# More products on zeros, and v products streamed twice, in the first batch of a fused attention and FFN kernel

## The chip, the cores and the metric

The kernel runs on one core of one Trainium2 chip. The metric is the device time of one execution in microseconds (us), the median over several executions. A profile of one execution tells how its time is spread over the engines: TensorE (PE, with its weight loads shown apart as PEld), VectorE (DVE), ScalarE (ACT), GpSimd (POOL) and the DMA queues that SyncE (SP) and POOL issue.

## The reference

For 4 batches of 8 heads with 768 positions of width 64, an 8x8 matrix per head is normalised by five rounds of exp, row sum and column sum (Sinkhorn). It mixes blocks of 96 keys and of 96 values: these are the "sorted" k and v. Each block of 96 queries then attends to its sorted block, and the result goes through a feed-forward net with squared ReLU.

```python
P = sort_net
for _ in range(5):
    P = np.exp(P - np.max(P, axis=-1, keepdims=True))
    P = P / (np.sum(P, axis=-1, keepdims=True) + 1e-09)
    P = P / (np.sum(P, axis=-2, keepdims=True) + 1e-09)
k_sorted = np.einsum('bhij,bhjcd->bhicd', P, k_b)
v_sorted = np.einsum('bhij,bhjcd->bhicd', P, v_b)
attn = softmax(scale * q_b @ k_sorted.T)          # per block of 96
x = (attn @ v_sorted) as [B * S, H * D]
out = (s * relu(x @ w_in) ** 2 + b) @ w_out
```

## The kernel before, in words

All work is written out in one order by hand (a manual schedule), and each engine runs its instructions in that order. A batch has two tiles of 384 positions, t = 0 to 7 over the four batches.

PSUM is shared by two pools of rotating buffers: `psa`, three buffers of two banks, and `psb`, two buffers of one bank. A new tile of a pool takes over a buffer, and its first write waits until all work on the tile that held it before is over.

The start of the program is about batch 0:

- `warm_up(n)` issues n matmuls of a 128x128 block of zeros with 256 columns of zeros (tile `zt`) into tiles `wp` of `psb`, one new tile for each. Nothing reads them.
- The Sinkhorn rounds run on DVE and ACT (lines 181 to 201).
- `q_half(half, eng)` transposes half of q of batch 0 on TensorE (`tq`, L244) and evicts it to `qt` on ACT.
- `build_pd1` spreads the normalised matrix over partitions with one f32 product (`pe`, L213), then builds the block-diagonal matrix `pd1` on DVE.
- `k_piece` makes sorted k: products `tk` (L278), evicted to `ks` by DVE ("v") or ACT ("s").
- `v_piece0(d0, n, eng)` makes sorted v of batch 0: for each of n columns of the head dimension one product `tv` (L304) of a strided slice of `vb` (64 rows, 128 columns) with the 64 columns of `pd1`, each into its own 64 columns of PSUM; then one eviction to `vs`.
- `s_piece(t, hp)` makes the scores of a head pair (`sc`, L359) and their exp on ACT (`at`, L362). `p_piece` multiplies them with v (`pv`, L386), and DVE divides (L390, L391) into `x`. `t_piece` transposes `x` (`tr`, L414) to `xt`.
- `ffn1` is the first FFN product (`hps`, L433) with its ReLU on ACT (L437) and square on DVE (L438); `ffn2` the second (`ops`, L459). Both call "slots" in between, in which pieces of the next batch are placed.

v of batch 1 takes another way: `v_piece1` multiplies, evicts to `vn` and writes to DRAM (`dv`, L326, on SP's queue); `v_read(1, nc.sync)` reads it back in another layout (`vs<-dv`, L345). The p pieces of tile 2, in a slot of `ffn2(0)`, are the first to need it. Loads of q, k, v and of the weights go by POOL's queue, each behind the last use of the buffer that it fills.

Of the kernel before, what the change touches and what calls it, by code (L numbers as in the profile page):

```python
# [9 lines left out]
FP = mybir.dt.float32  # L10
# [8 lines left out]
def kernel(  # L19
# [12 lines left out]
    nc = tc.nc  # L32
# [33 lines left out]
    psa = ctx.enter_context(tc.tile_pool(name="psa", bufs=3, space=bass.MemoryType.PSUM))  # L66
    psb = ctx.enter_context(tc.tile_pool(name="psb", bufs=2, space=bass.MemoryType.PSUM))
# [7 lines left out]
    vb = const.tile([128, 128, D], BF)  # L75
# [67 lines left out]
    for c0 in range(0, d_ff, FCH):  # L143
        w = const.tile([128, NHP, FCH], BF, name=f"wi{c0}")
        nc.gpsimd.dma_start(
            out=w, in_=moe_w_in.rearrange("(hp p) f -> p hp f", p=128)[:, :, c0:c0 + FCH])
# [19 lines left out]
    jsel = const.tile([128, NB], FP)  # L166
    ks = const.tile([128, 64, BLK], BF)

    def warm_up(n):
        for _ in range(n):  # L170
            wp = psb.tile([128, 256], FP, tag="b", name="wp")
            nc.tensor.matmul(out=wp, lhsT=zt[:, 0:128], rhs=zt, start=True, stop=True)  # L172

    def zero_pad(r0):
# [59 lines left out]
    def q_half(half, eng):  # L234

        if half == 0:
            QT[0] = qtp.tile([128, NHP, S], BF, tag="qt", name="qt0")
        pr = slice(half * 64, half * 64 + 64)
        ps = psa.tile([128, 2, 1024], BF, tag="a", name="tq")
        for hp in range(NHP):  # L240
            for t in range(TQ):
                c0 = (hp % 2) * TG + t * 64
                for e in range(2):
                    nc.tensor.transpose(out=ps[e * 64:(e + 1) * 64, hp // 2, c0:c0 + 64],  # L244
                                        in_=qr[0][pr, 2 * hp + e, t, :], identity=ident[pr, pr])
        for a in range(2):
            evac(QT[0][:, 2 * a:2 * a + 2, half * TG:(half + 1) * TG].rearrange(
                     "q b (p t) -> q b p t", t=TQ),
                 ps[:, a, 0:2 * TG].rearrange("q (b t p) -> q b p t", b=2, t=TQ), eng)
# [15 lines left out]
    def k_piece(b, c0, nc2, nb, eng):  # L265

        pr = brows(b)[1] if nb == 1 else slice(0, 128)  # L270
        rhs = (pd1[pr].rearrange("p e m i -> p (e m i)") if nb == 1
               else pd2.rearrange("p b e m i -> p (b e m i)"))
        if nc2 * nb > 8:
            ps = psa.tile([128, nc2, nb * 64], FP, tag="a", name="tk")
        else:
            ps = psb.tile([128, nc2, nb * 64], FP, tag="b", name="tk")
        for c in range(nc2):
            nc.tensor.matmul(out=ps[:, c, :],  # L278
                             lhsT=kb[pr, c0 + 2 * c:c0 + 2 * c + 2, :].rearrange("p c d -> p (c d)"),
                             rhs=rhs, start=True, stop=True)  # L280
        g0 = (b % 2) * 32

        def half(cp):
            if b == 0:
                cs = slice(c0 + cp, c0 + 2 * nc2, 2)
            else:
                cs = slice(cp * (BLK // 2) + c0 // 2, cp * (BLK // 2) + c0 // 2 + nc2)
            for e in range(2):
                evac(ks[e * 64:(e + 1) * 64, g0:g0 + nb * 32, cs].rearrange(
                         "p (b g) c -> p b g c", b=nb),  # L290
                     ps[cp * 64:(cp + 1) * 64].rearrange(
                         "p c (b e g) -> p e b g c", b=nb, e=2)[:, e], eng)

        half(0)
        return lambda: half(1)

    def v_piece0(d0, n, eng):

        if n > 8:
            ps = psa.tile([128, n, 64], FP, tag="a", name="tv")  # L300
        else:
            ps = psb.tile([128, n, 64], FP, tag="b", name="tv")
        for t in range(n):
            nc.tensor.matmul(out=ps[:, t, :], lhsT=vb[0:64, :, d0 + t],  # L304
                             rhs=pd1[0:64].rearrange("p e m i -> p (e m i)"),
                             start=True, stop=True)
        evac(VS[0][:, :, d0:d0 + n], ps[0:BLK].rearrange("p t g -> p g t"), eng)


# [40 lines left out]
    def s_piece(t, hp):  # L350

        b, half = divmod(t, 2)
        g0 = (b % 2) * 32 + hp * NB + half * HB
        sc = psa.tile([BLK, 2, 512], FP, tag="a", name="sc")
        for n in range(HB):
            for e in range(2):
                pr = slice(e * 64, (e + 1) * 64)
                q0 = (half * HB + n) * BLK
                nc.tensor.matmul(out=sc[:, e, n * BLK:(n + 1) * BLK], lhsT=ks[pr, g0 + n, :],  # L359
                                 rhs=QT[b][pr, hp, q0:q0 + BLK], start=True, stop=True)  # L360
        at = atp.tile([BLK, 2, TG], BF, tag="at", name="at")
        nc.scalar.activation(out=at, in_=sc[:, :, 0:TG], func=AF.Exp, scale=scale)  # L362
        AT[t, hp] = at

    def p_piece(t, hp, n0=0, nn=HB):

        b, half = divmod(t, 2)
        at = AT[t, hp]
        if t not in X:
            X[t] = xp.tile([BLK, HB, d_model], BF, tag="x", name="x")  # L370
        x = X[t]
        atf = at.rearrange("p e t -> p (e t)")
        if nn < HB:
            p1 = psb.tile([128, 512], FP, tag="b", name="pv")
            pv = [p1[:, e * nn * VW:(e + 1) * nn * VW] for e in range(2)]
            pvv = p1[0:BLK, 0:2 * nn * VW].rearrange("p (e n w) -> p e n w", e=2, w=VW)
        else:
            p2 = psa.tile([128, 2, 512], FP, tag="a", name="pv")
            pv = [p2[:, 0], p2[:, 1]]
            pvv = p2[0:BLK, :, 0:nn * VW].rearrange("p e (n w) -> p e n w", w=VW)  # L380
        for e in range(2):
            for n in range(n0, n0 + nn):
                c0 = (e * HB + n) * BLK
                m = 128 if c0 + 128 <= 2 * TG else BLK
                gi = e * 32 + hp * NB + half * HB + n
                nc.tensor.matmul(out=pv[e][0:m, (n - n0) * VW:(n - n0 + 1) * VW],  # L386
                                 lhsT=atf[:, c0:c0 + m],
                                 rhs=VS[b][:, gi, :], start=True, stop=True)
        rec = rtp.tile([BLK, 2, HB], FP, tag="rec", name="rec")
        nc.vector.reciprocal(out=rec[:, :, 0:nn], in_=pvv[:, :, :, D])  # L390
        nc.vector.tensor_tensor(  # L391
            out=x[:, n0:n0 + nn, hp * 128:(hp + 1) * 128].rearrange("p n (e d) -> p e n d", e=2),
            in0=pvv[:, :, :, 0:D],
            in1=rec[:, :, 0:nn].unsqueeze(3).broadcast_to([BLK, 2, nn, D]), op=ALU.mult)

    def t_piece(t, eng, n0=0, nn=HB):

        x = X[t]
        if t not in XT:
            XT[t] = xtp.tile([128, NHP, TG], BF, tag="xt", name="xt")  # L400
        if nn < HB:
            t1 = psb.tile([128, 1024], BF, tag="b", name="tr")
            tr = [t1[:, hp * nn * BLK:(hp + 1) * nn * BLK] for hp in range(NHP)]
            src = t1[:, 0:NHP * nn * BLK]
            dst = XT[t][:, :, n0 * BLK:(n0 + nn) * BLK]
            src = src.rearrange("p (a t) -> p a t", a=NHP)
        else:
            t2 = psa.tile([128, 2, 1024], BF, tag="a", name="tr")
            tr = [t2[:, hp // 2, (hp % 2) * TG:(hp % 2 + 1) * TG] for hp in range(NHP)]
            src = t2[:, :, 0:2 * TG]  # L410
            dst = XT[t].rearrange("p (a b) t -> p a (b t)", b=2)
        for hp in range(NHP):
            for n in range(n0, n0 + nn):
                nc.tensor.transpose(out=tr[hp][:, (n - n0) * BLK:(n - n0 + 1) * BLK],  # L414
                                    in_=x[:, n, hp * 128:(hp + 1) * 128],
                                    identity=ident[0:BLK, 0:BLK])
        evac(dst, src, eng)
# [91 lines left out]
    def build_pd1():  # L509
        pt = block_rows(0)  # L510
        nc.vector.tensor_tensor(  # L511
            out=pd1, in0=hmask.rearrange("p (m e) i -> p e m i", e=2),
            in1=bass.AP(tensor=pt.tensor, offset=pt.offset,
                        ap=[list(pt.ap[0]), [0, 2], [0, NHP], list(pt.ap[1])]),
            op=ALU.mult)
# [11 lines left out]

    warm_up(38)
    q_half(0, "s")
    warm_up(12)  # L530
    build_pd1()
    k_piece(0, 0, 16, 1, "v")()
    k_piece(0, 32, 16, 1, "s")()
    k_piece(0, 64, 8, 1, "v")()
# [3 lines left out]
    v_piece0(32, 16, "v")  # L538
    s_piece(0, 0)
    s_piece(0, 1)  # L540
    v_piece0(48, 16, "v")
    s_piece(0, 2)
    s_piece(0, 3)
    q_half(1, "s")
    for hp in range(NHP):
        p_piece(0, hp, 0, 2)
    t_piece(0, "v", 0, 2)
    s_piece(1, 0)
    s_piece(1, 1)

# [105 lines left out]
```

The softmax here doesn't subtract the row's maximum and nothing guards it: scores larger than these inputs give would overflow.

## Time and profile before

| what | value |
|---|---|
| median of 6 executions | 249.31 us (248.58 to 252.93) |
| the profiled execution's own time | 252.93 us |
| its span, first to last instruction | 251.2 us |
| mean granted TensorE clock | 0.952 |
| TensorE busy | 234.8 us (93%) |
| DVE, ACT busy | 133.3 us (53%), 116.4 us (46%) |

The profiled execution is the longest of the six. In the rows of the profile, a line such as "9.59 2.02 PE L172 MATMUL wp<-zt 128*128 128x256 bf16 x12" is: start in us from the span's start, length of the group in us, engine, line of the kernel, operation, tile written and tiles read, rows and columns of the weights, shape that streams, and the number of instructions. A bracket at its end gives the engine's idle time before the group and what ended it. In the forty slices of the page, a digit is a tenth: of busy time for an engine, of full speed for the granted clock (PEclk; 9 is 0.9 or more).

### The profile page before, as it was taken

To read this page: it belongs to the slowest core of one execution; us is meant where nothing else is said; L and a number is where in the kernel's file an instruction comes from. 1 tells how busy PE (TensorE), PEld (TensorE's weight loads), DVE (VectorE), ACT (ScalarE), POOL (GpSimd) and SP (SyncE) were. 2 spreads that over 40 slices of the span, in tenths; PEclk is the share of its full clock that TensorE was granted. 3 is DMA by queue.
4 is the path that set the end of the run, shared out by engine and by line. 5 is a ranking of instruction groups with operands and counts; after the bars stand their busy time and mean duration, and the time that the engine had idled before them with its cause. 6 is when DMAs were issued, how large, how long until landed. Compare 5 with 4: busy or idle time off the path is not lost.

```text
span 251.2 us, 4978 instructions
## 1 busy us (share of the span) xinstructions
PE 234.8 (93%) x2128; PEld 141.4 (56%) x2128; DVE 133.3 (53%) x260; ACT 116.4 (46%) x156; POOL 39.3 (16%) x51
## 2 busy tenths in 40 slices
PE   8879799799999699989899999999999999999993
PEld 4578699645544355655555555665555555664441
DVE  4776556999991236547774535344364353442221
ACT  5346566335358153677754141666431536661000
POOL 7720200588800007200000000000000000000000
PEclk9955579999999799999999999999999999999999
DMA  4999999999759936995001121100012110000122
GB/s 62 188 195 212 213 201 206 207 207 232 135 116 121 316 125 69 154 153 90 0 1 44 51 77 42 44 0 0 4 42 82 46 68 18 3 0 35 49 83 85
DMA packets 20214, 24.97 MB, mean 99 GB/s; under 512 B 7520, under 2 KB 14432, under 8 KB 19680
## 3 DMA queue, kind: packets, MB, share of 16 engines
q0 software_dynamic: 8400, 15.21, 35.5%
q1 hardware_dynamic: 11792, 9.45, 14.6%
q8 instruction: 16, 0.26, 0.5%
q14 instruction: 6, 0.05, 0.1%
HBM read 29.63 MB, written 8.65 MB: 152 GB/s over the span
## 4 chain that ended last, share of the span: by engine, by line
PE 69%; DVE 12%; DMA 9%; ACT 6%; issue 1%; SPq 1%; DVEq 0%
PE ops L459 29%; PE hps L433 27%; DMA vs<-dv 5%; PE pv L386 4%; DVE gt L438 3%; DMA dv<-vn 3%; ACT rt L437 3%; PE sc L359 3%; PE tr L414 2%; ACT ks L230 2%; PE tv L304 2%; DVE ks L228 1%; DVE qt L228 1%; PE tk L278 1%; DMA sn<-in_sort_net_dram 1%
## 5 line engine op out<-in xcount | busy, mean ns | idle before, releaser
L459 PE MATMUL ops<-wo,gt 128*128 128x512 bf16 x384 | 91.6, 383 | 0.0
L433 PE MATMUL hps<-xt,wi 128*128 128x384 bf16 (+1 forms) x576 | 89.2, 311 | 2.4 <-ACT ks L230 1.1
L433 PEld LDWEIGHTS <-wi 128*128 128x128 bf16 x576 | 54.3, 99 | 31.7 <-issue 4.1
L437 ACT ACTIVATE rt<-hps 128x768 bf16<-128x768 f32 (+1 forms) x72 | 53.3, 740 | 38.1 <-PE hps L433 34.4
L438 DVE TENSOR_TENSOR gt<-rt 128x768 bf16<-128x768 bf16 (+1 forms) x72 | 43.0, 601 | 43.1 <-ACT rt L437 42.8
L459 PEld LDWEIGHTS <-gt 128*128 128x128 bf16 x384 | 35.3, 99 | 39.1 <-issue 1.7
L450 DVE SCALAR_TENSOR_TENSOR ot<-ops,s_bc,bias 128x512 f32<-128x512 f32 x24 | 18.0, 748 | 36.4 <-PE ops L459 36.4
L362 ACT ACTIVATE at<-sc 96x768 bf16<-96x768 f32 x32 | 24.2, 802 | 24.1 <-PE sc L359 24.1
L391 DVE TENSOR_TENSOR x<-pv,rec 96x512 bf16<-96x512 f32 (+1 forms) x36 | 22.6, 628 | 1.3
L230 ACT COPY xt<-tr 128x1536 bf16<-128x1536 bf16 x6 | 8.6, 1439 | 23.6 <-PE tr L414 23.6
L228 DVE CAST ks<-tk 64x512 bf16<-64x512 f32 (+1 forms) x28 | 18.6, 664 | 1.7 <-PE tk L278 1.3
L390 DVE RECIPROCAL rec<-pv 96x8 f32<-96x8 f32 (+1 forms) x36 | 6.9, 193 | 20.6 <-PE pv L386 20.6
L583 POOL TENSOR_TENSOR csum<-csum,wo 128x512 f32<-128x512 f32 x14 | 17.6, 1255 | 1.0
L230 ACT CAST ks<-tk 64x512 bf16<-64x512 f32 (+1 forms) x24 | 14.0, 582 | 7.1 <-PE tk L278 6.8
L386 PEld LDWEIGHTS <-at 96*128 96x128 bf16 (+1 forms) x256 | 12.2, 105 | 7.5 <-DMA vs<-dv 3.1
L386 PE MATMUL pv<-vs,at 96*128 96x66 bf16 (+1 forms) x256 | 13.1, 201 | 3.4 <-DMA vs<-dv 2.6
L359 PEld LDWEIGHTS <-ks 64*96 64x96 bf16 x256 | 8.4, 132 | 6.1 <-issue 5.0
L359 PE MATMUL sc<-qt,ks 64*96 64x96 bf16 x256 | 10.8, 223 | 0.3 <-DVE ks L228 0.2
L172 PE MATMUL wp<-zt 128*128 128x256 bf16 x50 | 9.7, 323 | 1.1 <-DVE warm L104 1.1
L230 ACT CAST vn<-tv 128x1024 bf16<-128x1024 f32 x6 | 6.1, 1012 | 8.5 <-PE tv L334 8.3
L345 POOL DMA_DIRECT2D vs<-dv x4 | 5.4, 1348 | 24.9 <-DMA dv<-vn 23.5
L278 PE MATMUL tk<-pd,kb 64*128 64x64 bf16 (+1 forms) x144 | 8.3, 216 | 0.9 <-DVE pd L511 0.9
(67 smaller groups left out, 120.6 us busy)
## 6 DMA issues: line engine op xcount, KB each, us to landing
out_dram<-ot SPq DMA_DIRECT2D x24, 256.0 KB, 2.0
kb<-in_k_dram POOLq DMA_DIRECT2D x4, 768.0 KB, 22.4
vb<-in_v_dram POOLq DMA_DIRECT2D x4, 768.0 KB, 19.3
qr<-in_q_dram POOLq DMA_DIRECT2D x3, 768.0 KB, 36.4
wi<-in_moe_w_in_dram POOLq DMA_DIRECT2D x2, 1024.0 KB, 18.9
wo<-in_moe_w_out_dram POOLq DMA_DIRECT2D x2, 1024.0 KB, 30.5
dv<-vn SPq DMA_DIRECT2D x6, 256.0 KB, 3.5
vs<-dv POOLq DMA_DIRECT2D x4, 384.0 KB, 11.2
```

The lines of the kernel that those rows point to most:

```text
L228: nc.vector.tensor_copy(out=out, in_=in_)
L230: nc.scalar.copy(out=out, in_=in_)
L359: nc.tensor.matmul(out=sc[:, e, n * BLK:(n + 1) * BLK], lhsT=ks[pr, g0 + n, :], rhs=QT[b][pr, hp, q0:q0 + BLK], start=True, stop=True)
L362: nc.scalar.activation(out=at, in_=sc[:, :, 0:TG], func=AF.Exp, scale=scale)
L386: nc.tensor.matmul(out=pv[e][0:m, (n - n0) * VW:(n - n0 + 1) * VW], lhsT=atf[:, c0:c0 + m], rhs=VS[b][:, gi, :], start=True, stop=True)
L391: nc.vector.tensor_tensor(out=x[:, n0:n0 + nn, hp * 128:(hp + 1) * 128].rearrange("p n (e d) -> p e n d", e=2), in0=pvv[:, :, :, 0:D], in1 ...
L433: nc.tensor.matmul(out=hps[:, f, 0:nt], lhsT=wi_at(hp, f0 + f), rhs=xt[:, hp, c0:c0 + nt], start=(hp == 0), stop=(hp == NHP - 1))
L437: nc.scalar.activation(out=rt[:, :, 0:nt], in_=hps[:, :, 0:nt], func=AF.Relu)
L438: nc.vector.tensor_tensor(out=gt[:, f0:f0 + 2, c0:c0 + nt], in0=rt[:, :, 0:nt], in1=rt[:, :, 0:nt], op=ALU.mult)
L450: nc.vector.scalar_tensor_tensor(out=ot, in0=ops, scalar=s_bc, in1=bias, op0=ALU.mult, op1=ALU.add)
L459: nc.tensor.matmul(out=ops, lhsT=gt[:, f, m * 128:(m + 1) * 128], rhs=wo_at(f), start=(f == 0), stop=(f == NF - 1))
L583: nc.gpsimd.tensor_tensor(out=csum, in0=csum, in1=wo_at(f), op=ALU.add)
```

## The change

Only batch 0's part, before the first `ffn1`, is touched. `warm_up` takes one tile for all its matmuls, of `psb` or, where asked, of `psa`. The number of matmuls on zeros grows: 22 instead of 12 after the first q half, 9 more between the f32 product of `build_pd1` and the first k piece, 6 before the last v piece, 6 before the second q half, and 2 in `psa` after each of the four p pieces and after the t piece. In `v_piece0` each product streams the 64 columns of `pd1` twice in a row (a broadcast access) and writes 128 columns of PSUM: its own 64 and the 64 of the next product, which then overwrites them. The last product of each eight streams once.

```diff
-    def warm_up(n):
+    def warm_up(n, pool=psb):
+        wp = pool.tile([128, 256], FP, tag="b" if pool is psb else "a", name="wp")
         for _ in range(n):
-            wp = psb.tile([128, 256], FP, tag="b", name="wp")
             nc.tensor.matmul(out=wp, lhsT=zt[:, 0:128], rhs=zt, start=True, stop=True)
...
         for t in range(n):
-            nc.tensor.matmul(out=ps[:, t, :], lhsT=vb[0:64, :, d0 + t],
-                             rhs=pd1[0:64].rearrange("p e m i -> p (e m i)"),
-                             start=True, stop=True)
+            r = 2 if t % 8 < 7 else 1
+            nc.tensor.matmul(out=ps[:, t:t + r, :], lhsT=vb[0:64, :, d0 + t],
+                             rhs=pd1[0:64].rearrange("p e m i -> p (e m i)").unsqueeze(1)
+                             .broadcast_to([64, r, 64]), start=True, stop=True)
...
     warm_up(38)
     q_half(0, "s")
-    warm_up(12)
+    warm_up(22)
     build_pd1()
+    warm_up(9)
     k_piece(0, 0, 16, 1, "v")()
     k_piece(0, 32, 16, 1, "s")()
...
     s_piece(0, 0)
     s_piece(0, 1)
+    warm_up(6)
     v_piece0(48, 16, "v")
     s_piece(0, 2)
     s_piece(0, 3)
+    warm_up(6)
     q_half(1, "s")
     for hp in range(NHP):
         p_piece(0, hp, 0, 2)
+        warm_up(2, psa)
     t_piece(0, "v", 0, 2)
+    warm_up(2, psa)
     s_piece(1, 0)
     s_piece(1, 1)
```

## The prediction

> **What bounds the kernel now.** I read the page's busy times and its forty slices first, then a table of the first 40 us in windows, then the timeline there, last the waits behind it. Page: TensorE is the bound over the span, and its clock is halved in slices 3 to 5 and partly in 14.
>
> ```profile
> PE 234.8 (93%) x2128; PEld 141.4 (56%) x2128; DVE 133.3 (53%) x260; ACT 116.4 (46%) x156; POOL 39.3 (16%) x51
> PEclk9955579999999799999999999999999999999999
> ```
>
> Windows: start and end, their length, each engine's busy time, and after the five engines the granted clock.
>
> ```profile
> 10.00:15.00 5.00, 3.21 (x36) 2.38 (x36) 2.61 (x13) 1.62 (x3) 2.12 (x3) 0.85 0.98 203
> 15.00:20.00 5.00, 4.34 (x60) 4.16 (x57) 4.84 (x9) 4.22 (x7) 0.54 (x1) 0.50 1.18 207
> 30.00:35.00 5.00, 5.00 (x60) 4.52 (x58) 1.83 (x6) 2.49 (x4) 0.88 (x1) 0.60 1.19 191
> 35.00:40.00 5.00, 5.00 (x81) 4.43 (x78) 3.70 (x13) 3.73 (x8) 0.00 (x0) 1.00 1.23 204
> ...
> 82.00:84.00 2.00, 0.01 (x1) 0.01 (x1) 0.00 (x0) 0.00 (x0) 0.00 (x0) 1.00 1.24 281
> 86.00:88.00 2.00, 2.00 (x6) 0.76 (x5) 0.23 (x1) 1.01 (x1) 0.00 (x0) 0.50 0.76 283
> ```
>
> A mean of 0.85 over 10 to 15 puts the fall at 13.5 (1.5 us at half); 0.60 over 30 to 35 puts the rise at 34.0. So all of batch 0 before the FFN runs at half clock, 20.5 us. A second, single stretch of about 3.4 us (85.2 to 88.6) follows a TensorE wait; 20.5 is six times 3.4, so I take it (estimate) that the clock is decided every 3.4 us on the 3.4 us before.
>
> Timeline: start, length, engine, line, operation, count, idle time before and what ended it.
>
> ```profile
> 9.59 2.02 PE L172 MATMUL wp<-zt 128*128 128x256 bf16 x12
> 12.49 0.40 PE L213 MATMUL pe<-sn,emat 32*128 32x64 f32 x2 [0.88 <-DVE sn L201]
> 13.80 2.71 PE L278 MATMUL tk<-pd,kb 64*128 64x64 bf16 x48 [0.90 <-DVE pd L511]
> 16.77 1.62 PE L304 MATMUL tv<-pd,vb 64*128 64x64 bf16 x16 [0.26 <-DMA vb<-in_v_dram]
> 18.80 2.96 PE L304 MATMUL tv<-pd,vb 64*128 64x64 bf16 x32 [0.40 <-ACT ks L230]
> 23.07 1.38 PE L304 MATMUL tv<-pd,vb 64*128 64x64 bf16 x14 [0.57 <-ACT at L362]
> 25.94 1.49 PE L244 MATMUL tq<-ident,qr 64*64 64x64 bf16 x48 [0.64 <-DVE vs L228]
> 28.58 0.38 PE L386 MATMUL pv<-vs,at 96*128 96x66 bf16 x4 [0.60 <-DVE rec L390]
> 31.32 1.46 PE L433 MATMUL hps<-xt,wi 128*128 128x192 bf16 x8
> 34.99 0.83 PE L433 MATMUL hps<-xt,wi 128*128 128x192 bf16 x8
> ...
> 83.99 0.71 PE L386 MATMUL pv<-vs,at 96*128 96x66 bf16 x16 [2.59 <-DMA vs<-dv]
> ```
>
> To be seen: eight FFN products take 1.46 us at half clock and 0.83 at full; TensorE's waits between 11 and 31 us are short (0.2 to 1.15) and end on DVE or ACT; and the end of batch 1's v (vs<-dv, back from DRAM) is the next place where TensorE stands still.
>
> **What makes the clock fall.** I counted, per 3.4 us, the time in which columns stream (columns over 2.4 per ns at full clock: cold wp start every 0.213 us for 256 columns, and half that warm). 10.1 to 13.5 has 9 wp of 0.107 and the f32 product, 33%: it falls. 81.8 to 85.2 has 32%: it falls. 47.6 to 51.0 has 49%: it stays. Cold, 13.5 to 16.9 has 77% and does not rise; 30.6 to 34.0 has 94% and rises. The Trainium skill (TensorE: Matmul & The Clock Gate, "Why this matters for your kernels") says the clock halves after gaps of over some 3 us between bursts, one idle window. By that rule no gap here is long enough (the longest before 13.5 is 0.9 us), nothing would fall, and filling short waits would be worth 0. The rows decide: a window one third full fell. I take 0.4 of streaming as the edge, between 0.33 and 0.49.
>
> **The change part by part.**
> *Warm-ups in one tile.* Now each wp takes a fresh buffer of two and waits for the product two before: 168 ns each warm (12 in 2.02), 202 over the 38. With one tile that wait goes; I take 107 to 110 warm (stream only), 213 cold (as now). If the rewriting of the same bank waited for each end instead, the price is a whole product, 269 ns warm and 371 cold by its rows: the upper bound, and a rival. I take the stream, since accumulating products (ops L459) rewrite one bank back to back with no wait. The 38 then end near 8.0 instead of 8.8 (26 cold to 6.7, 12 x 0.11), q half 0 starts 0.7 earlier (its load has landed by 7.2), and nobody needs it before ACT at 10.8: 0.
> *22 for 12, and 9 after pd's product.* 22 x 0.11 = 2.4 us, 8.95 to 11.35, before the Sinkhorn result at 12.4: hidden. Nine take 1.0 from 12.75 against pd at 13.75: hidden to within 0.1; cold they would be 1.9 and put 1.0 on the path. Windows now: about 60% in 10.1 to 13.5, about 50% in 13.5 to 16.9 (9 wp rest, 48 tk x 27 ns): above 0.4, so no fall.
> *k products.* 53 ns each now, 29 warm (16 in 0.64 at 66.6 us, less the last one's 0.19). Second piece ready 0.6 to 0.7 earlier; ACT's four evictions (15.70 to 18.75) move by that, so v's second piece starts at 18.2 (behind the first, which stays on its DMA at 16.77) instead of 18.80: -0.6.
> *v streamed twice.* 88 ns each now ((2.96 - 0.27)/31) although 64 columns stream in 53: the strided weight load bounds it. Doubled, 128 columns are 107 cold and 53 warm. Warm it hides under 88 (cost 0); if the load follows the clock, a product falls to about 54 and a piece gains another 0.5; cold, +19 ns x 16 = 0.3 a piece. I take 0 (no row shows this load warm). Its streaming share becomes 60% instead of 30%.
> *Six warm-ups before v's last piece and six before q half 1.* Warm 0.65 each in waits of 0.85 (22.2 to 23.07) and 0.9 (25.0 to 25.94): hidden. Cold 1.28: +0.45 each. With DVE's evictions 0.5 earlier, q half 1 starts near 25.45 (-0.5); its 48 transposes take 0.95 (as at 8.71) instead of 1.49: -1.1 at the first p piece.
> *Two warm-ups in psa after each p piece and after t.* 0.22 each. They take PSUM buffers of psa: by rotation the third needs q half 1's, which ACT empties 1.5 us after the transposes (27.9): p piece 3 waits about 0.2 more behind it. DVE's pace (0.55 a piece) hides the rest; bound 0 to 0.5, I take 0.2. First FFN product at about 30.3 instead of 31.32: -1.0.
> *FFN until 34.0.* Two rounds at 1.4 cold against about 0.9: -1.0.
> Sum: 2.0 us earlier at 34 us. The profiled execution rose as early as it could (the FFN filled the window from 30.6); where the decision falls later in that window the old kernel loses up to 1.7 more, +0.6 as an estimate. So 2.0 to 2.6.
> *What is late next.* From 34 to 81 TensorE is nearly always busy, so the shift goes through. POOL's loads of the next batches are issued earlier too, but the DMA engines are full until 67 (share about 1), so that moves nothing. Batch 1's v goes out in twelve writes, the last landing near 70.7 with the tail of the loads, and comes back in 13 us (70.8 to 84). If writes move with their issue, all of the gain stays; if they end with the loads, none does. Their latency (8.4 us) is a full queue's, which moves with the issue: I take 0.75 of 2.3 = 1.7.
>
> **Base.** The profiled execution is 252.93 us (span 251.2, 1.7 around it), 3.6 over the median of 249.31; its second clock stretch costs at most 1.7 of that. The stage changed precedes both, so I take the 1.7 off the median: 247.6.
>
> **Rivals.**
> A, *the clock falls all the same* (26%): if activity counts rows as well as columns, k and v products on 64 of 128 rows count half, and 16.9 to 20.3 would stand at 0.27 and 13.5 to 16.9 at 0.32, where 0.28 (the same count in 10.1 to 13.5) fell and 0.43 (47.6 to 51.0) stayed. The rows fit this as well as they fit columns. Then the wp run at 213 ns: +0.45 twice, v +0.3 twice, +0.5 to 0.9 around the p pieces, less 0.6 already gained and an earlier rise: +0.5 to +2, so 249.8 to 251.3, slower. It decides from a fall before about 24 us.
> B, *the wait at vs<-dv takes it* (17%): v's return stays at its time, TensorE idles 2 us longer before the p pieces of tile 2; 249.3, and where that wait leaves a window under 0.4, up to 1.7 of half clock more, 251.0. For: the last writes land with the last load (70.0). Against: latency as above.
> C, *rewriting a tile waits* (7%): 38 x 0.43 alone puts q half 0 at 17.4, v 64 x 0.2 more: over 260. Against: the accumulating rows.
> The forecast itself: 50%.
>
> **Numbers.** No change means within 0.2% (0.5 us), about what measuring this kernel can tell. Forecast: 246.3 to 248.7 on its own (v's load following the clock below, half the shift lost above). Faster: 0.50 plus a little of A and B where the rise comes early or half is lost, 0.52. Same: half of B and a part of A, 0.14. Slower: most of A, the rest of B, C, 0.34. Range 246.4 to 251.4: it leaves out C and thin ends.
>
> **What would show it.** Right: clock 1.0 from about 6.7 to the wait before tile 2's p pieces; tk in about 1.6 us; tv pieces of 16 still near 1.4; q half 1 in 0.95; first hps at 30.3; everything at 50 us two us earlier. Wrong: 0.5 anywhere in 13 to 30 (A); the same start of the pv at 84 with a longer idle before it (B); wp rows started over 250 ns apart (C).

## The result, and the profile after

The changed kernel takes 249.50 us (median of 34 executions, 248.19 to 251.47), the kernel before 248.98 us (71 executions, 247.84 to 253.30). The ratio is 1.0030, 95% interval 1.0015 to 1.0045: slower by 0.3%, where 0.7% faster had been forecast. Ratios, and the counts of executions by their clock below, leave out executions more than 1.5% above the fastest of the same kernel. The profiled execution of after took 249.45 us, with a span of 247.7 us. The 251.2 us span of the profile shown of before is at the long end of its executions, so a second trace of the kernel before (span 247.6 us, 249.3 us in all) is used below wherever times within the span are compared. It is called "before, second trace".

The page of after: busy time of each engine, and the granted TensorE clock in forty slices of 6.2 us.

```profile
PE 234.8 (95%) x2169; PEld 143.6 (58%) x2169; DVE 133.1 (54%) x260; ACT 116.3 (47%) x156; POOL 39.3 (16%) x51
PEclk9995599999999999999999999999999999999999
```

The clock still falls. The table of windows tells where (start and end, length, busy time of PE, PEld, DVE, ACT and POOL, then the granted clock, the DMA share and GB/s).

```profile
12.00:15.00 3.00, 2.72 (x54) 2.30 (x55) 1.25 (x4) 0.12 (x1) 0.88 (x1) 1.00 0.94 194
15.00:18.00 3.00, 1.36 (x23) 1.27 (x20) 2.91 (x6) 2.94 (x5) 0.54 (x1) 1.00 1.21 202
18.00:22.00 4.00, 4.00 (x51) 4.00 (x51) 2.64 (x5) 2.75 (x5) 0.00 (x0) 0.52 1.13 212
26.00:30.00 4.00, 4.00 (x72) 3.07 (x69) 1.37 (x3) 2.32 (x4) 1.09 (x3) 0.50 1.11 228
30.00:34.00 4.00, 3.96 (x56) 2.99 (x54) 2.50 (x8) 1.72 (x3) 0.85 (x1) 0.78 1.14 192
```

From 18 to 30 us TensorE is never idle, 4.00 of 4.00 in each window, and the clock is at half all the same. The trace's own clock records give the fall at 18.14 and the rise at 31.80. The timeline of the same stretch shows what TensorE did there:

```profile
8.10 2.58 PE L172 MATMUL wp<-zt 128*128 128x256 bf16 x22
12.31 1.16 PE L172 MATMUL wp<-zt 128*128 128x256 bf16 x9
13.74 1.57 PE L278 MATMUL tk<-pd,kb 64*128 64x64 bf16 x48 [0.28 <-DMA kb<-in_k_dram]
16.95 4.72 PE L306 MATMUL tv<-pd,vb 64*128 64x128 bf16 x46 [1.64 <-DMA vb<-in_v_dram]
22.43 1.46 PE L172 MATMUL wp<-zt 128*128 128x256 bf16 x6
23.82 1.68 PE L306 MATMUL tv<-pd,vb 64*128 64x128 bf16 x14
26.26 1.46 PE L172 MATMUL wp<-zt 128*128 128x256 bf16 x6
27.65 1.49 PE L244 MATMUL tq<-ident,qr 64*64 64x64 bf16 x48
29.29 0.62 PE L172 MATMUL wp<-zt 128*128 128x256 bf16 x2
33.14 0.82 PE L435 MATMUL hps<-xt,wi 128*128 128x192 bf16 x8
```

Three things are to be seen. The k products take 1.57 us instead of 2.71 (2.18 in the second trace), so they end 1.2 us sooner (0.65 against the second trace), and TensorE then stands still for 1.64 us because v's load lands where it did before (16.95, against 16.77 and 16.85). The two groups of six zeros run at half clock, 1.46 us each with the last one's tail, in places where the kernel before waits 0.57 and 0.64. And the first FFN product starts at 33.14 us.

Rows of before, second trace, for the same places:

```profile
13.78 2.18 PE L278 MATMUL tk<-pd,kb 64*128 64x64 bf16 x48 [0.90 <-DVE pd L511]
16.85 4.42 PE L304 MATMUL tv<-pd,vb 64*128 64x64 bf16 x48 [0.89 <-DMA vb<-in_v_dram]
22.53 1.42 PE L304 MATMUL tv<-pd,vb 64*128 64x64 bf16 x14 [0.57 <-ACT at L362]
25.43 1.49 PE L244 MATMUL tq<-ident,qr 64*64 64x64 bf16 x48 [0.64 <-DVE vs L228]
30.81 1.46 PE L433 MATMUL hps<-xt,wi 128*128 128x192 bf16 x8
```

Against these, each step comes out so (the last column is what the step added to after's lateness):

| start, us | before, second trace | after | step added |
|---|---|---|---|
| scores behind v's third piece | 21.08 | 21.37 | 0.29 |
| last v piece | 22.53 | 23.82 | 1.00, the first six |
| scores behind it | 23.67 | 25.20 | 0.24, v streamed twice |
| q half 1 | 25.43 | 27.65 | 0.69, the second six |
| first FFN product | 30.81 | 33.14 | 0.11, the pairs |
| 33rd FFN product | 35.97 | 36.81 | -1.49 |
| p pieces of tile 2 | 82.04 | 82.18 | -0.70 |

So 2.33 us are lost up to the FFN. 1.49 us come back there, since after's clock rises at 31.80 and the other's at 34.94; another 0.70 come back by tile 2, 0.54 of it a wait for batch 1's v that the kernel before has and after has not. The rows of tile 2, before (second trace) and then after:

```profile
82.04 0.71 PE L386 MATMUL pv<-vs,at 96*128 96x66 bf16 x16 [0.54 <-DMA vs<-dv]
```

```profile
82.18 0.70 PE L388 MATMUL pv<-vs,at 96*128 96x66 bf16 x16
```

What is left at tile 2 in these two traces is 0.14 us. Over all executions 0.5 us is left.

### The profile page after: what moved, and what is told of

Same layout as the page of the kernel before. It is cut to its first block, busy times and chain, and to the rows that moved or that the text cites. A ratio compares the mean times of both kernels' runs of the same rounds, so it can differ in the third digit from the quotient of the medians.

```text
span 247.7 us, 5058 instructions
## 1 busy us (share of the span) xinstructions
PE 234.8 (95%) x2169; PEld 143.6 (58%) x2169; DVE 133.1 (54%) x260; ACT 116.3 (47%) x156; POOL 39.3 (16%) x51
## 4 chain that ended last, share of the span: by engine, by line
PE 79%; DVE 8%; DMA 6%; ACT 4%; issue 1%; POOL 1%; POOLq 0%
PE ops L461 33%; PE hps L435 28%; DMA vb<-in_v_dram 6%; PE pv L388 4%; PE sc L361 3%; ACT rt L439 3%; PE tv L306 3%; DVE gt L440 2%; DVE ks L228 2%; PE tr L416 2%; PE wp L172 2%; DVE qt L228 1%; PE tq L259 1%; PE tv L336 1%; ACT ks L230 1%
## 5 line engine op out<-in xcount | busy, mean ns | idle before, releaser
L461 PE MATMUL ops<-wo,gt 128*128 128x512 bf16 x384 | 90.5, 379 | 0.0
L435 PE MATMUL hps<-xt,wi 128*128 128x384 bf16 (+1 forms) x576 | 88.0, 308 | 2.5 <-ACT ks L230 1.1
L435 PEld LDWEIGHTS <-wi 128*128 128x128 bf16 x576 | 53.4, 98 | 31.6 <-issue 4.1
L172 PE MATMUL wp<-zt 128*128 128x256 bf16 x91 | 15.5, 329 | 1.1 <-DVE warm L104 1.1
L172 PEld LDWEIGHTS <-zt 128*128 128x128 bf16 x91 | 9.7, 115 | 3.4 <-DVE warm L104 1.1
L228 DVE COPY qt<-tq 128x1536 bf16<-128x1536 bf16 x4 | 7.0, 1754 | 3.5 <-PE tq L259 3.5
L347 POOL DMA_DIRECT2D vs<-dv x4 | 5.4, 1348 | 20.5 <-DMA dv<-vn 19.1
```

Source lines behind the costliest of these rows:

```text
L228: nc.vector.tensor_copy(out=out, in_=in_)
L435: nc.tensor.matmul(out=hps[:, f, 0:nt], lhsT=wi_at(hp, f0 + f), rhs=xt[:, hp, c0:c0 + nt], start=(hp == 0), stop=(hp == NHP - 1))
L461: nc.tensor.matmul(out=ops, lhsT=gt[:, f, m * 128:(m + 1) * 128], rhs=wo_at(f), start=(f == 0), stop=(f == NF - 1))
```

## What the clock counts

In every trace the clock's changes lie on a grid of 3.413 us: 18.14 less 4.49 (after's first rise) is four times that. The Trainium skill (TensorE: Matmul & The Clock Gate, "What's actually happening") gives that window and says that it runs freely; here its phase against the program differs from trace to trace: where the clock rises at the start, it does so between 3.78 and 6.99 us.

For each such window I counted, from the instructions of a trace, the time in which a matmul streams: its columns divided by 2.4 per ns, or by 1.2 at half clock. Each product is weighted by the share of the array that its weights take: rows over 128 times columns over 128. Products that overlap in time (transposes, scores) add up in this array share; in the plain streaming time the overlap counts once. This count is my own; the profile has no such row. Over the first 100 us of after, both traces of before and the other 15 experiments, the array share parts the windows without one exception:

```
array share in a window   what the clock did at its end
full, 0.10 to 0.36        fell (22 windows)
full, 0.39 and more       stayed
half, up to 0.75          did not rise
half, 0.77 and more       rose
```

Streaming time without the rows, which is what the prediction counted, doesn't part them: windows fell at up to 0.56 and stayed at 0.44. Rows alone, with overlapping products added up, don't either: half-clock windows at 0.90 did not rise, others at 0.78 did. With overlap counted once, though, rows alone part the falls as well (0.36 fell, 0.39 stayed) and nearly part the rises (0.73 did not rise, 0.71 did). So the windows show that rows count; that the columns of the weights do is less certain. In after, the window from 14.73 to 18.14 holds the rest of k, the wait, and the start of v: 0.31 of streaming, 0.15 of the array. The next one, all v, streams 0.97 of the time at half clock but stands at 0.51 of the array, and doesn't rise.

## The experiments

The theories: R, a product counts by the rows and columns of its weights and the time it streams, so v on 64 rows stands too low even when it streams twice; C, streaming time alone counts, whatever the rows; H, the fall comes from the hole ahead of v's load alone; and for the end of the time, whether the return of batch 1's v gives back what was lost or won.

**Zeros in the hole.** To after, 16 zeros between k and v:

```diff
     k_piece(0, 80, 8, 1, "s")()
+    warm_up(16)
     v_piece0(0, 16, "v")
```

> The changed kernel with 16 more matmuls on zeros between the last k piece and the first v piece, where TensorE waited 1.6 us for v's load while the clock was still full. Theory R (activity counts rows as well as columns: 64 of 128 rows is half): the window that fell at 18.1 now holds about 0.7 and the clock stays up there, but the next one is v products alone (0.3 by rows and columns) and falls, near 21.5: TensorE's first FFN product at 32 to 33 us, time 0.999 to 1.003 of the kernel before. Theory C (columns alone count, the 1.6 us hole was all): v streamed twice holds 0.6, the clock stays full to 80 us, first FFN product near 30.3, time 0.990 to 0.995.

Measured: 1.0309 (1.0281 to 1.0337). The experiment put itself in the way. Its tile takes a buffer of `psb`, and both were held by the last two k pieces until these had been evicted; the wait ended on ACT (timeline):

```profile
19.57 3.57 PE L172 MATMUL wp<-zt 128*128 128x256 bf16 x16 [4.35 <-ACT ks L230]
23.07 4.44 PE L306 MATMUL tv<-pd,vb 64*128 64x128 bf16 x46
```

So it says nothing on the filled hole. It gives one window for R: after a rise at 23.48, the window to 26.90 holds v streamed twice at full clock and no wait (streaming 0.56, array 0.28), and the clock fell.

**The two halves of the change.** After with each v product streamed once (`r = 1`), and before with v streamed twice and none of the new zeros:

> The changed kernel with v's products streamed once, as before: the matmuls on zeros alone. If the zeros at half clock are what costs (41 more, 0.213 us each cold, in waits of 0.2 to 0.9 us), the first FFN product stays near 33 us and the time at 1.001 to 1.004 of before. If it is v streamed twice (107 ns instead of 88 cold, 64 of them, 1.2 us), it comes at about 32 and the time at 0.997 to 1.001.

> The kernel before with v's products streamed twice and nothing else. The clock is at half from 13.5 anyway. Theory R: 0.5 a window does not bring it back; each piece of 16 takes 1.65 instead of 1.4 us, but the first two stand beside DVE's and ACT's evictions: first FFN product 0.3 to 0.8 later than the 31.3 of before, time 1.001 to 1.003. Theory C: v's windows are full of columns and bring the clock back at 20 to 24, first FFN product at or before 31.3, time 0.994 to 1.000.

Measured: zeros alone 1.0017 (0.9993 to 1.0040), v twice alone 1.0025 (1.0008 to 1.0042). Neither part gains anything. The trace of zeros alone starts the FFN at 33.53, near 33 as expected if the zeros at half clock are what costs. That of v twice alone starts it at 31.01, only 0.20 behind before, second trace, where 0.3 to 0.8 behind the first had been expected. In this trace the three half-clock windows that hold v stream for 0.76 to 0.81 of the time, 0.41 to 0.43 of the array, and the clock doesn't rise in any.

**Zeros on 64 rows.** Before, with its first 38 zeros on half of the rows, the columns unchanged:

```diff
-            nc.tensor.matmul(out=wp, lhsT=zt[:, 0:128], rhs=zt, start=True, stop=True)
+            nc.tensor.matmul(out=wp, lhsT=zt[0:rows, 0:128], rhs=zt[0:rows], start=True, stop=True)
...
-    warm_up(38)
+    warm_up(38, 64)
```

> The kernel before with the first 38 matmuls on zeros on 64 of the 128 rows (same 256 columns, same pace: 0.213 us each at half clock). Nothing else changes. Theory R: half the activity, no rise: wp stays at 371 ns through the 38, which end near 9.3 us, and the clock is at half until the FFN at 31 to 35 us. Theory C: as before, the clock rises at 4.5 to 8 us and later wp take 269 ns.

One execution: 249.63 us. The timeline:

```profile
5.84 3.57 PE L172 MATMUL wp<-zt 64*128 64x256 bf16 x16
9.34 1.49 PE L244 MATMUL tq<-ident,qr 64*64 64x64 bf16 x48
15.03 2.71 PE L278 MATMUL tk<-pd,kb 64*128 64x64 bf16 x48 [0.90 <-DVE pd L511]
32.55 1.46 PE L433 MATMUL hps<-xt,wi 128*128 128x192 bf16 x8
```

The zeros stream nine tenths of the time for over 7 us and never raise the clock: transposes, k products and the first FFN products all run at half. It first rises at 34.98, in the FFN. Streaming time alone (C) is refuted as what raises it.

**Without the sixes, and without the pairs too.** After without both `warm_up(6)` and with v streamed once; then also without the `warm_up(2, psa)` lines:

> The changed kernel without its two groups of six matmuls on zeros and with v streamed once; one tile, 38, 22 and 9 at the start and the pairs between the p pieces stay. If the sixes and v streamed twice are what pushed the FFN back (six are 1.28 us cold against waits of 0.85 and 0.9; v 0.3 a piece), q half 1 starts at or before 25.9 as in the kernel before, the first FFN product at 31.0 to 31.6, and with the earlier rise that the pairs bring (31 to 32 us instead of 34) the time is 0.995 to 0.999 of before. If the pairs cost as much as they bring, 0.999 to 1.002.

> The same without the pairs too: only one tile and 38, 22 and 9. The k products run at full clock (1.6 instead of 2.7 us), the clock falls in v's part, the FFN's first window brings it back. First FFN product 0 to 0.4 earlier than 31.3, time 0.998 to 1.001. If the start alone slowed the changed kernel, it would be above 1.002.

Measured: 0.9983 (0.9964 to 1.0001), and 1.0004 (0.9982 to 1.0026). The zeros at the start, in one tile, and the pairs are the better part of the change, though no gain of theirs is clear of the noise. Against zeros alone (1.0017, of another session) the sixes cost 0.34%. Without the sixes the first FFN product starts at 30.52 and the clock rises at 29.49, so the FFN has it from the start; without the pairs as well it starts at 30.43, but the clock rises at 35.41. The pairs bring the rise forward, as they fill a half-clock window to 0.83 of the array. Their worth in the time is smaller than the two intervals can tell. And at 34 to 70 us the kernel without sixes is 1.78 us ahead of before, second trace, but only 0.97 at tile 2:

```profile
81.07 0.71 PE L387 MATMUL pv<-vs,at 96*128 96x66 bf16 x16 [1.35 <-DMA vs<-dv]
```

**Zeros in v's own tile.** The first experiment mended: the 16 zeros write the PSUM tile of the first v piece, which it is to overwrite, so nothing new is waited for.

```diff
+        if d0 == 0:
+            for _ in range(16):
+                nc.tensor.matmul(out=ps[:, 0:4, :], lhsT=zt[:, 0:128], rhs=zt,
+                                 start=True, stop=True)
         for t in range(n):
```

> The changed kernel with 16 matmuls on zeros written into the first v piece's own tile ahead of its products, so that they wait for no other buffer. They fill 15.1 to 16.9 us. Theory R (rows times columns, falls at 0.36 or less of a 3.4 us window, stays at 0.41): the window up to 18 stays up, the next, v alone at 88 ns with half of the rows, stands at 0.3 and falls, at 20 to 22 us; first FFN product 32 to 33 us, time 0.999 to 1.003. Theory C: the clock stays full to 80 us, time 0.990 to 0.995.

Measured: 1.0042 (1.0019 to 1.0065).

```profile
15.14 1.92 PE L306 MATMUL tv<-zt 128*128 128x256 bf16 x16
16.99 4.38 PE L310 MATMUL tv<-pd,vb 64*128 64x128 bf16 x46
22.13 1.46 PE L172 MATMUL wp<-zt 128*128 128x256 bf16 x6
32.86 0.82 PE L439 MATMUL hps<-xt,wi 128*128 128x192 bf16 x8
```

The hole is gone and the clock falls one window later, at 21.37, behind a window (17.96 to 21.37) of streaming 0.56 and array 0.29. So the hole is not the whole cause: in this trace v at half of the rows is enough for the fall. The hole has a part in it all the same. In 9 of these 21 executions the mean clock is 0.993 or more, so it can't have stayed at half through batch 0; none of the 35 of after is above 0.990, and 32 are at 0.972 or less. Where the grid cuts v's stretch, so that each window also holds some of the zeros or scores beside it, the clock can hold at half of the rows.

**Zeros between v's products.** The same kernel with a zero after each second v product, to lift v's windows:

```diff
+            if t % 2 and t < 12:
+                zeros(4 if t < 4 else 12)
```

> The changed kernel with zeros also in v's part: 16 ahead of the first piece and 6 among the products of each piece, all in the piece's own tile. By rows times columns a window of v now stands at about 0.5, above the 0.41 that stayed. Theory R: the clock stays full from its rise to 80 us; the zeros lengthen each piece by 0.65 us, v's last piece starts near 24.5, q half 1 near 28, first FFN product 31.5 to 32.7 with the FFN at full clock at once: 0.998 to 1.003. A wrong theory R would show half clock between 17 and 30.

Measured: 1.0502 (1.0450 to 1.0555), a miss.

```profile
16.81 0.40 PE L313 MATMUL tv<-pd,vb 64*128 64x128 bf16 x2
17.14 0.28 PE L305 MATMUL tv<-zt 128*128 128x256 bf16 x1
17.36 0.39 PE L313 MATMUL tv<-pd,vb 64*128 64x128 bf16 x2
```

Two products and a zero have a period of 0.54 us at full clock, where their streaming is 0.21 and two products alone take 0.18: each change between them costs time, for a reason that was not looked for. The window stood at 0.33 of the array and fell at 19.77, and the FFN starts only at 44.42.

**The load of batch 2's q.** The kernel before once more; then before, after, and after without the sixes and with v once, each with `load_q(2)` moved:

```diff
     load_k(*brows(2))
-    load_q(2)
...
     ffn2(0, qu)
     load_k(*brows(3))
+    load_q(2)
```

> The kernel before, unchanged, for a second trace of it. The profile shown before held a wait of 2.6 us for batch 1's v and a second half-clock stretch after it. If that was peculiar to the one execution, this one has no such wait, the clock is at half from about 13 to 17 until 31 to 37 us alone, and the span is 246 to 247.5 us.

> The kernel before with batch 2's q loaded later: its load stands behind batch 3's k instead of ahead of batch 3's v, so the DMA tail that now ends at 67 to 70 us is 1.6 MB shorter, some 6 to 8 us. Theory L (the twelve writes of batch 1's v land with the tail of the loads, whenever they were issued, and their return holds TensorE): they land by about 63, the read starts 4 to 6 us earlier, no wait before tile 2's p pieces; 0.5 us less than before, and none of the executions above 251: 0.996 to 0.999. Theory Q (the writes have a fixed latency of 8 us behind their issue): no change, 0.999 to 1.002.

> The changed kernel with the same later load. Theory L: the wait at tile 2 that hid part of the changed kernel's lateness is gone from both, so against the before kernel with the late load it is slower by the whole 0.9 us and more that it is late at 34 us (0.3 to 0.6%); against the kernel before itself 1.000 to 1.003. Theory Q: as without the later load, 1.002 to 1.005.

> The changed kernel without the sixes and with v streamed once, with the same later load. It was 1.8 us ahead at 34 us and lost 0.8 of that in a wait of 1.35 us for batch 1's v. Theory L: no wait there, the whole gain reaches the end: 0.991 to 0.995 of before. Theory Q: 0.997 to 0.999 as without it.

Measured: before with the load moved 0.9985 (0.9968 to 1.0002), after 1.0062 (1.0034 to 1.0091), without the sixes 0.9963 (0.9943 to 0.9982). The reads of batch 1's v wait for its last writes; these are their rows on SP's queue (L345 to L347, times of the first and the last issue), first before (second trace), then without the sixes, then before with the load moved:

```profile
L345 SPq DMA_DIRECT2D vs<-dv x2: 337/1920/3503, 68.6 to 69.0; - x2
```

```profile
L346 SPq DMA_DIRECT2D vs<-dv x2: 337/2048/3759, 68.8 to 69.2; - x2
```

```profile
L345 SPq DMA_DIRECT2D vs<-dv x2: 334/1160/1987, 64.9 to 65.2; - x2
```

Products issued 1.8 us sooner moved the writes' end not at all; a transfer less ahead of them moved it by 3.7 us. The writes' own times say how. The first of the twelve is issued at 51.44 in before (second trace) and at 49.66 without the sixes, and lands at 58.81 and 58.84. The ninth is issued at 58.88 and 58.90, right behind that landing. These are the waits of SP's queue on its own writes, in the same two kernels:

```profile
SPq L326 <- DMA dv<-vn: 2.2, 1, 2.2
```

```profile
SPq L327 <- DMA dv<-vn: 3.0, 1, 3.0
```

So an earlier first write lands no earlier, and the last four are issued hardly earlier either (the twelfth at 60.81 and 60.67). In none of the three kernels with the load moved does TensorE wait at tile 2. With that wait gone nothing hides the change's own loss, and it stands at 1.0062 against 0.9985. Part of this difference is the clock: of after with the load moved, 9 of 16 executions have a mean of 0.965 or less, and 14 of 35 with the load in its old place. The two parts were not separated. The gain of the kernel without sixes was half of the one expected; which part of it is lost was not found.

**The rows alone.** v of batch 0 gets a tile of its own whose other 64 rows are cleared on POOL, and its products take all 128 rows. The sums are the same, the columns are the same, and only the rows double. The tile of its own also frees `vb` sooner for the next loads, which the control below shares. The base is the kernel with 16 zeros in v's own tile.

```diff
+    nc.gpsimd.memset(vb0[64:128, 0:BLK, :], 0.0)
     load_q(1)
...
-            nc.tensor.matmul(out=ps[:, t:t + r, :], lhsT=vb[0:64, :, d0 + t],
-                             rhs=pd1[0:64].rearrange("p e m i -> p (e m i)").unsqueeze(1)
-                             .broadcast_to([64, r, 64]), start=True, stop=True)
+            nc.tensor.matmul(out=ps[:, t:t + r, :], lhsT=vb0[0:128, :, d0 + t],
+                             rhs=pd1[0:128].rearrange("p e m i -> p (e m i)").unsqueeze(1)
+                             .broadcast_to([128, r, 64]), start=True, stop=True)
```

> The kernel with 16 zeros ahead of the first v piece in its own tile, and v of batch 0 in a tile of its own whose other 64 rows are cleared (by POOL, ahead of the load of batch 1's q); the v products of batch 0 take all 128 rows of it, so the same columns stream on twice the rows, and the sums are the same. Theory R (activity is rows times columns): the window that stood at 0.29 and fell at 21.4 stands near 0.57, so the clock holds to the FFN; v pieces at 88 ns a product (1.4 us for 16; 1.7 if a weight load of 128 rows takes longer), the sixes 0.65 instead of 1.46, q half 1's transposes 0.95, first FFN product at 30.0 to 30.9 against 32.86; of these 2 to 2.8 us about half is left after batch 1's v: 0.994 to 1.000 of before. Theory C (columns alone count): falls at about 21.4 as with half the rows, first FFN product near 32.9, 1.003 to 1.006.

> Control of the full-rows kernel: the same tile of its own and the same clearing, but the v products on the 64 rows of v. Both theories: as the kernel with 16 zeros in v's own tile (clock falls near 21.4 or, in other phases of the grid, 18; first FFN product 32.7 to 33.3; 1.002 to 1.007 of before). If the clearing on POOL slows DVE ahead of the k products, everything is up to 0.5 us later, here and with full rows.

The clock of the full-rows kernel in forty slices, then that of its control (same tile, same clearing, 64 rows):

```profile
PEclk9999999999999999999999999999999999999999
```

```profile
PEclk9996589979999999999999999999999999999999
```

The control fell at 19.95, behind a window of 0.55 streaming and 0.30 array. With all rows the windows of v stand at 0.71 and 0.59 of the array, and the clock never falls. The timeline of the full-rows kernel:

```profile
17.03 4.43 PE L313 MATMUL tv<-pd,vb 128*128 128x128 bf16 x48
21.89 0.83 PE L175 MATMUL wp<-zt 128*128 128x256 bf16 x6
22.68 1.57 PE L313 MATMUL tv<-pd,vb 128*128 128x128 bf16 x16
24.67 0.83 PE L175 MATMUL wp<-zt 128*128 128x256 bf16 x6
25.46 0.95 PE L247 MATMUL tq<-ident,qr 64*64 64x64 bf16 x48
30.00 0.82 PE L442 MATMUL hps<-xt,wi 128*128 128x192 bf16 x8
81.15 0.71 PE L395 MATMUL pv<-vs,at 96*128 96x66 bf16 x16 [1.96 <-DMA vs<-dv]
```

The sixes hide now (0.83 with the tail), q half 1 takes 0.95, and the FFN starts at 30.00, against 33.34 in the control. From 34 to 70 us this trace is 3.15 us ahead of after's, and 2.31 ahead of before, second trace (33rd FFN product at 33.66 against 35.97). Then it waits 1.96 us for v where that one waits 0.54, and 0.89 are left (81.15 against 82.04). In the times: 0.9982 (0.9944 to 1.0020), the control 1.0013 (0.9990 to 1.0036). The intervals of these two overlap, so the times don't part them. The clock does, and not only in the two traces: none of the 13 executions with full rows has a mean below 0.986, and 9 of the control's 17 are at 0.979 or less. A half-clock window takes 0.007 from the mean, so 0.986 leaves room for two; the control's fall in batch 0 lasts four. The control also tells what a held clock is worth: its 8 executions at 0.984 or more have a median of 248.5 us, the 9 others 250.4.

**The same with the wait gone, and with v streamed once.**

> The full-rows kernel with the load of batch 2's q moved behind that of batch 3's k, which took the wait for batch 1's v away before. Theory R: the 2 to 2.8 us won by 34 us stay to the end, no wait at the p pieces of tile 2: 0.988 to 0.995 of before, the fastest kernel of all. If the gain at 34 us is there but the end moves by less than half of it, something behind 50 us takes it. Theory C: as the kernel after with this load moved, 1.004 to 1.008.

> The full-rows kernel with each v product streaming once: 128 rows, half the columns, the same product of both as twice on 64 rows. Theory R: as with half the rows, a window of v alone stands at 0.29 and the clock falls at 18 to 21.5; sixes 1.46; first FFN product 32 to 33; 1.000 to 1.005. If rows weigh more than columns (activity is rows switched on while busy), it holds the clock as the full-rows kernel does: first FFN product 30 to 31.

Full rows with batch 2's q loaded later: 0.9885 (0.9833 to 0.9938), medians 247.11 against 249.05 us. It is the fastest of all the kernels, and beats both before and after.

```profile
29.63 0.82 PE L442 MATMUL hps<-xt,wi 128*128 128x192 bf16 x8
79.92 0.70 PE L395 MATMUL pv<-vs,at 96*128 96x66 bf16 x16
```

It is 2.67 us ahead of before, second trace, at 34 us (33rd FFN product at 33.30 against 35.97). A single half-clock window at 47.2 to 50.6 takes 1.25 of that. The 1.42 that remain all pass tile 2, where no wait takes them, and the wait that the other trace has there adds 0.70: 2.12 us in all (79.92 against 82.04), which stay to the end (span 245.5 against 247.6).

Full rows with each product streamed once: 0.9966 (0.9928 to 1.0005). The expected fall did not come: the first FFN product starts at 30.00.

```profile
17.15 4.35 PE L313 MATMUL tv<-pd,vb 128*128 128x64 bf16 x48
```

The window of the expectation, nothing but v, would stand at 0.30. In this trace the grid lies so that v shares its windows with zeros, and the lowest has 0.41, so the trace alone fits R. The executions together don't. If R's count were right, each position of the grid with a window of v at 0.36 or less would bring a fall. Sliding the grid over the four traces gives the share of such positions, an estimate from the starts and shapes of their products:

```
v of batch 0 (16 zeros ahead)       positions with a fall   mean clock 0.979 or less
64 rows, twice, v's old tile         0.71                    12 of 21 executions
64 rows, twice (the control)         0.45                    9 of 17
128 rows, twice                      0                       0 of 13
128 rows, once                       0.56                    0 of 10
```

The first three agree with R; the last does not. None of its ten executions is below 0.986. On all rows, v streamed once held the clock although by R's count it stands no higher than v twice on half of the rows (0.30 for both). So streaming twice wasn't needed, and R's count by streaming time is too low for such a product. The rows are shown to matter; what a product counts for while it streams less than its turn takes is not known.

## Why the prediction was wrong

*The step that failed* is the edge under "What makes the clock fall": 0.4 of streaming time, whatever the rows. The prediction said itself that the rows fitted rows times columns as well, and put that in rival A. It took 0.60 for v streamed twice and so above the edge, but on half of the rows (0.28 to 0.30 of the array) that did not hold the clock: with the hole filled, the same columns on all rows kept a mean of 0.986 or more in 13 of 13 executions, on half of the rows 9 of 17 fell to 0.979 or less. Rival A, that rows count, is what happened; its further sum, rows times streaming time, is not borne out by v once on all rows. Its price, +0.5 to +2 us, holds the +0.5 measured, at its low end because the earlier rise gave back 1.5 us and 0.7 more came back by tile 2. Its absolute figures, 249.8 to 251.3, start from a median of six that was 0.3 us above that of 71, and miss the 249.50.

*A second omission in the same part.* Its two windows, "about 60%" and "about 50%", were worked for the grid of one execution, and left out the 1.64 us in which TensorE waits for v's load once k is done sooner. In this execution that hole alone would have made the window fall (0.31 by the prediction's own count). With the hole filled, the fall came one window later in the trace, and did not come in 9 of 21 executions. So both errors had the same sign.

*"What is late next"* was wrong too. It let 0.75 of a shift through, on the ground that writes move with their issue. The reads behind them were issued at 68.6 and 68.8 us in two kernels 1.8 us apart, and at 64.9 with one load fewer ahead: the writes end with the loads, which is rival B's mechanism. Of 1.78 us, 0.97 came through without the sixes, of 2.31 with full rows 0.89, and, once the load of batch 2's q was out of the way, all that the second half-clock window had left. Since the shift had the other sign here, the same wait softened the loss.

*Point by point, what held.* Zeros in one tile: 0.11 us apart at full clock (2.58 us for 22, less the last one's tail), no wait for rewriting, so rival C is out. k products 29 ns against the 29 forecast. v streamed twice: about 90 ns a product at full clock and 107 at half, as the bounds had it, hence +0.24 us for a piece of 16 (0.3 forecast). The sixes at half clock: +1.0 and +0.69 where +0.45 each was forecast for that case; the waits they fill were taken as 0.85 and 0.9, where the rows of both traces have 0.57 and 0.64 of idle time. The pairs: 0.11 against 0.2.

*The gain of a held clock was there.* With full rows the first FFN product starts at 30.00 us (forecast 30.3) and the trace is 2.31 us ahead of before, second trace, at 34 us (2.0 to 2.6 forecast). What was mistaken is that this change holds the clock, not what a held clock is worth: within the control it is worth 1.9 us (248.5 against 250.4).

*What stays open.* That the columns of the weights count as the rows do rests on which windows fell and rose, and on how overlapping products are counted, not on an experiment of its own. Why v streamed once on all rows never fell is not explained. Full rows without the zeros in the hole were not tried. One window of the p pieces and v (array 0.27 to 0.36, near 47 to 51 us) falls in some executions and not in others, with the grid's phase; nothing was tried to lift it, though it took 1.25 us in the fastest kernel's trace.

## What to carry to other kernels

To keep TensorE's clock, look per 3.4 us at how many rows of the array are at work and for how long, and not only at how long TensorE is busy. Do it for every phase of the grid, and count the holes that a faster stage leaves ahead of a load that doesn't move. Judge by the mean clock of many executions, since one trace shows one phase. A product on half of the rows can be given the other half as zeros at no cost in TensorE time that shows here (about 90 ns a v product either way; clearing the tile took POOL 5.2 us, before v was needed); zeros pushed between the products did cost time. And before a gain upstream is booked, look for the next transfer that ends with the DMA backlog: in this kernel it decided how much of the gain arrived.

## What the runs showed of the hardware

- Half clock needs no idle window, against the rule that the prediction quotes. The clock fell behind a window whose longest wait was 0.9 us (10.1 to 13.5 in the profile shown of before), and behind one with no wait at all (v at 0.29 of the array). In the traces, to rise took 0.77 and more of the array, to stay 0.39: between the two the clock kept what it had, so a single bad window cost as long as the work behind it stayed under 0.77 (four windows, 13.65 us, in after).
- The phase of the grid differs in each execution, and with it the time: executions of after with a mean clock of 0.978 to 0.990 have spans of 246.5 to 246.7 us, those at 0.970 to 0.972 247.2 to 248.1, those at 0.952 have 249.5 to 249.8. A change that only shifts the place of the fall shows in some executions and not in others.
- A v product, with its strided weights, takes about 90 ns a turn, whether on 64 rows or 128, and at full clock whether it streams 64 columns or 128 ((4.43 - 0.19)/47 = 90 on 128 rows, 128 columns; (4.35 - 0.19)/47 = 89 on 128 rows, 64 columns). At half clock 64 columns on 64 rows take 88 ((4.42 - 0.27)/47), 128 columns on 64 rows 107.
- A write on SP's queue that is issued sooner need not land sooner: the first of batch 1's twelve landed at 58.81 and 58.84, issued 1.78 us apart, and in both kernels the ninth was issued only behind that landing.
- Zeros and products that take turns in one PSUM tile cost 0.54 us for two products and a zero, where the same instructions in runs of their own take 0.29 (0.18 and 0.11). The cause was not looked for.
